# A three-layer kernel issued by its own list scheduler, with the order of its weight preparation changed

## The chip, the cores and the metric

The kernel runs on one core of a Trainium2 chip. The metric is the time of the whole program on the device in microseconds, as the median of several runs. The core has five engines that work side by side, each on its own queue in order: PE (matrix multiplication, with weight loads that overlap it), DVE and ACT (element-wise work), POOL, and SP, which issues the DMAs.

## The reference

Attention is a linear recurrence over 768 steps for 4 batches and 8 heads of width 48; its result is the input of two feed-forward layers over 3072 tokens.

```
mag = sqrt(a_re^2 + a_im^2);  scale = min(mag, 0.999) / (mag + 1e-6);  a = (a_re + i a_im) * scale
S_t = a_t * S_(t-1) + k_t v_t^T          # S: 48 x 48, complex, per batch and head
y_t = q_t^T re(S_t)
x  = y as (3072, 384)
x  = relu(x @ w_in)^2 @ w_out            # d_ff 2048
out = (silu(x @ w_gate) * (x @ w_val)) @ w_out2   # d_ff 1536
```

All inputs and outputs are float32.

## The kernel before

The sequence is cut into 6 chunks of 128 steps, 512 tokens each. For a chunk `attention` runs two generators: `elem` (DVE and ACT: normalisation, running products of a, scaled q and k called qs and ks, for two pairs of heads at a time) and `mat` (PE: transposes of ks and qs to kT and qT, copied by ACT; scores sc, masked by DVE to pb; py; the state). Its result goes by ACT (ys, L372) and DMA into xf. `moe1` splits xf into a high and a low part (xh, xl, L474 and L475) and then takes 16 column tiles of w_in: nine matmuls for h, Relu and Square (u), a rounded copy (gh, ACT), the remainder (gl, DVE L515), and two iterations later nine matmuls of `down` into acc. Products are made in three parts, high by high, high by low and low by high, so that float32 is kept on a faster matrix type. `moe2` does the same with two matrices (pg, pv), Silu on ACT and 12 iterations; its input comes back from DRAM through `input2`.

A weight tile is prepared by `wsplit`: read as integers (wst), three DVE operations (L400, L402, L404) put together the low part of wt, ACT rounds it into the first half (L413; DVE at L411 when `late` is set, that is for the second layer), POOL subtracts for the second half (L414), and ACT makes two flags of it (L417, L418). `prep1` does so for the 32 tiles of the first layer, `prep2` for the 36 of the second. Split tiles lie in 32 slots `w`, and in slots of attention's tiles when that is over (`wspare`); the integers are read into three buffers `pp`, which attention's pp and Bt share.

The order in which work is written is set by `drain`, which advances several generators in proportion: attention of chunk 0 together with `prep1`; then for each chunk `moe1` with the attention of the next one; for the last chunk `moe1` with `prep2`, which has first been advanced by its 8 spare slots; then `moe2` chunk by chunk. The framework's scheduler takes this as priority, orders the instructions of each engine by a model of its own, gives tiles their slots and sets all waits.

## Time and profile before

| | us |
|---|---|
| median of 3 runs (1225.9 to 1233.1) | 1231.74 |
| profiled execution, its own time | 1228.35 |
| span of the profiled execution | 1226.6 |
| PE busy | 1082.4 |
| DVE busy | 760.1 |
| ACT busy | 637.7 |
| POOL busy | 97.5 |

The span is from the first to the last instruction. Busy time is the time in which at least one instruction of the engine runs; as matmuls are pipelined and overlap, a busy PE is not PE at its peak. PEclk is the share of the matrix clock that was granted: 1.00 is 2.4 GHz and 0.50 is 1.2 GHz. In the stretches used below, 0 to 265 us holds attention of chunks 0 and 1 and the first layer of chunk 0; 265 to 374, 374 to 476, 476 to 579 and 579 to 685 the first layer of chunks 1 to 4, each with the attention of the next chunk; 685 to 772 the first layer of chunk 5; and then come six chunks of the second layer.

### The profile page before, as it was taken

How to read it: one execution, taken by the hardware profiler on the slowest of the kernel's cores; microseconds unless marked ns; L12 is line 12 of the kernel's file. 1: busy time of each engine (PE TensorE's matmuls, PEld its weight loads, DVE VectorE, ACT ScalarE, POOL GpSimd, SP SyncE). 2: the span in 40 equal slices, each digit the busy share in tenths (PEclk: the TensorE clock that was granted, in tenths of full speed). 3: DMA queues.
4: the chain of work that ended last, by engine and by line, in shares of the span. 5: the costliest groups of instructions: out<-in, count | busy, mean ns of one | idle time of the engine just before them, and what ended most of it. 6: DMA issues, size and time to landing. Idle time of an engine off the chain costs nothing.

```text
span 1226.6 us, 16542 instructions
## 1 busy us (share of the span) xinstructions
PE 1082.4 (88%) x5842; PEld 901.6 (74%) x5842; DVE 760.1 (62%) x1566; ACT 637.7 (52%) x1280; POOL 97.5 (8%) x75
## 2 busy tenths in 40 slices
PE   0346589989999999999999877999999999999997
PEld 0235467767777877878778655788898888888886
DVE  7987597968879879879788799223232232222221
ACT  4666777657677677777768666212122121221211
POOL 1231240000000000000003344000000000000000
PEclk9955599989999999999999999999999999999999
DMA  5353523142233332332334443101000010000000
GB/s 141 100 144 115 166 81 104 49 129 65 68 107 88 91 92 70 112 102 65 104 91 142 151 133 104 52 1 52 1 26 28 1 52 1 26 1 1 26 1 29
DMA packets 102492, 89.27 MB, mean 73 GB/s; under 512 B 35072, under 2 KB 90368, under 8 KB 102400
## 3 DMA queue, kind: packets, MB, share of 16 engines
q1 hardware_dynamic: 102400, 88.12, 24.5%
q8 instruction: 48, 0.79, 0.3%
q14 instruction: 44, 0.36, 0.1%
HBM read 64.49 MB, written 18.87 MB: 68 GB/s over the span
## 4 chain that ended last, share of the span: by engine, by line
PE 59%; DVE 22%; ACT 10%; issue 6%; DMA 2%; POOL 1%; SPq 0%; DVEq 0%; ACTq 0%; POOLq 0%
PE pg L483 4%; PE acc L558 4%; PE acc L556 4%; PE pg L484 4%; PE acc L557 4%; PE pg L482 4%; PE pv L483 4%; PE pv L482 4%; PE pv L484 4%; PE sc L348 3%; PE py L367 3%; PE pu L386 2%; PE acc L498 2%; PE acc L499 2%; DVE wt L402 2%
## 5 line engine op out<-in xcount | busy, mean ns | idle before, releaser
L569 DVE TENSOR_TENSOR u<-pv,u 128x512 f32<-128x512 f32 x72 | 49.8, 692 | 208.4 <-PE pv L484 208.4
L571 ACT CAST gh<-u 128x512 fp32r<-128x512 f32 x72 | 44.7, 620 | 217.0 <-PE acc L557 191.9
L482 PE MATMUL h<-xh,wc 128*128 128x512 f32 x288 | 117.6, 411 | 19.9 <-ACT xh L474 12.2
L498 PE MATMUL acc<-gl,wr 128*128 128x512 f32 x288 | 117.0, 406 | 20.3 <-DVE gl L515 20.1
L483 PE MATMUL h<-xl,wc 128*128 128x512 f32 x288 | 117.0, 406 | 5.7 <-DVE xl L475 5.7
L572 DVE TENSOR_TENSOR gl<-u,gh 128x512 fp32r<-128x512 f32 x72 | 49.8, 692 | 109.7 <-ACT gh L571 109.7
L497 PE MATMUL acc<-gh,wr 128*128 128x512 f32 x288 | 113.4, 403 | 4.6 <-ACT gh L514 4.6
L484 PE MATMUL h<-xh,wc 128*128 128x512 f32 x288 | 116.5, 405 | 0.0
L499 PE MATMUL acc<-gh,wr 128*128 128x512 f32 x288 | 114.5, 398 | 0.0
L414 POOL TENSOR_TENSOR wc<-wt,wc 128x384 fp32r<-128x384 f32 x40 | 58.7, 1466 | 573.0 <-DVE wc L411 506.8
L558 PE MATMUL acc<-wr,gl 128*128 128x384 f32 x288 | 97.0, 337 | 0.0
L556 PE MATMUL acc<-wr,gh 128*128 128x384 f32 x288 | 96.9, 336 | 0.0
L557 PE MATMUL acc<-wr,gh 128*128 128x384 f32 x288 | 96.7, 336 | 0.0
L568 ACT ACTIVATE u<-pg 128x512 f32<-128x512 f32 x72 | 43.0, 598 | 98.3 <-PE pg L484 98.3
L515 DVE TENSOR_TENSOR gl<-u,gh 128x512 fp32r<-128x512 f32 x96 | 74.4, 777 | 18.0 <-ACT gh L514 17.5
L483 PE MATMUL pg<-xl,wc 128*128 128x512 f32 x216 | 85.0, 394 | 0.0
L484 PE MATMUL pg<-xh,wc 128*128 128x512 f32 x216 | 85.0, 394 | 0.0
L483 PE MATMUL pv<-xl,wc 128*128 128x512 f32 x216 | 84.2, 390 | 0.0
L482 PE MATMUL pv<-xh,wc 128*128 128x512 f32 x216 | 84.1, 390 | 0.0
L482 PE MATMUL pg<-xh,wc 128*128 128x512 f32 x216 | 84.1, 389 | 0.0
L484 PE MATMUL pv<-xh,wc 128*128 128x512 f32 x216 | 84.0, 389 | 0.0
L498 PEld LDWEIGHTS acc<-gl,wr 128*128 128x128 f32 x288 | 54.3, 189 | 40.1 <-DVE gl L515 29.5
(131 smaller groups left out, 2482.6 us busy)
## 6 DMA issues: line engine op xcount, KB each, us to landing
wst<-in_moe_w_out_dram SPq DMA_DIRECT2D x28, 384.0 KB, 3.1
scr<-ks SPq DMA_DIRECT2D x24, 384.0 KB, 2.5
kn<-scr SPq DMA_DIRECT2D x24, 384.0 KB, 3.6
wst<-in_moe_w_in_dram SPq DMA_DIRECT2D x16, 384.0 KB, 3.9
in<-in_a_re_dram SPq DMA_DIRECT2D x96, 48.0 KB, 1.9
in<-in_a_im_dram SPq DMA_DIRECT2D x96, 48.0 KB, 1.9
in<-in_k_dram SPq DMA_DIRECT2D x96, 48.0 KB, 2.2
in<-in_q_dram SPq DMA_DIRECT2D x96, 48.0 KB, 2.0
```

The lines of the kernel that those rows point to most:

```text
L414: nc.gpsimd.tensor_tensor(out=dst[:, 1], in0=x, in1=dst[:, 0].bitcast(F32), op=ALU.subtract)
L482: nc.tensor.matmul(ps, w[:, 0, kd], xh[kd], start=kd == 0, stop=False)
L483: nc.tensor.matmul(ps, w[:, 0, kd], xl[kd], start=False, stop=False)
L484: nc.tensor.matmul(ps, w[:, 1, kd], xh[kd], start=False, stop=kd == self.KD - 1)
L497: nc.tensor.matmul(acc[d], w[:, 0, d], gh, start=i == 0, stop=False)
L498: nc.tensor.matmul(acc[d], w[:, 0, d], gl, start=False, stop=False)
L499: nc.tensor.matmul(acc[d], w[:, 1, d], gh, start=False, stop=i == NF - 1)
L515: nc.vector.tensor_tensor(out=gl, in0=u, in1=gh.bitcast(F32), op=ALU.subtract)
L556: nc.tensor.matmul(acc[t], gh[:, ts], f(0), start=i == 0, stop=False)
L557: nc.tensor.matmul(acc[t], gh[:, ts], f(1), start=False, stop=False)
L558: nc.tensor.matmul(acc[t], gl[:, ts], f(0), start=False, stop=i == NF - 1)
L569: nc.vector.tensor_tensor(out=u, in0=pv, in1=u, op=ALU.mult)
```

## The change

All calls of the main path go to a recorder (`Plan`), which notes each instruction's tiles, what it depends on and a duration from `weigh`. `arrange` then plays the engines forward in time: an engine that is free takes, of the instructions that are ready and whose tiles have a slot, the one that was recorded first; tiles of one tag get slots in the order of their recording. `issue` emits the instructions in the resulting order under `manual_schedule`, in which the framework keeps the given order and only sets the waits.

The recording order changes too. Attention of chunk 0 is recorded alone, except that after its first 5 steps 8 weight tiles are read ahead (`READ`, `LOADS`); the 32 splits come after it, one pair of tiles ahead of each iteration of moe1 on chunk 0 (`behind`), beside attention of chunk 1. 24 of the 32 reads go into slots of tag `w` itself, the last 8 into `pp`. For the second layer, 8 tiles are advanced as before, 16 are recorded beside moe1 of the last chunk (`EARLY`) and the rest beside moe2 of chunk 0. In `wsplit` ACT always makes the rounded copy and DVE subtracts in POOL's place; the last chunk's square goes from DVE to ACT; the output tile of moe2's fourth row block takes a buffer of gl.

```diff
--- before.py
+++ after.py
@@ -18,6 +18,265 @@
+class Engine:
+    def __init__(self, plan, engine, name):
+        self.plan, self.engine, self.name = plan, engine, name
+    def __getattr__(self, method):
+        call = getattr(self.engine, method)
+        return lambda *a, **kw: self.plan.record(self.name, method, call, a, kw)
...
+    def record(self, engine, method, call, args, kw):
+        names = self.POSITIONS.get(method, ("out", "in_"))
+        full = dict(zip(names, args))
+        full.update(kw)
+        aps = {k: v for k, v in full.items() if isinstance(v, bass.AP)}
+        o = Op()
+        i = len(self.ops)
+        o.call, o.args, o.kw, o.engine, o.rank = call, args, kw, engine, i
+        o.after, o.order, o.users, o.frees, o.tiles, o.ready, o.pair, o.size = set(), set(), [], [], [], 0.0, None, 0
+        self.ops.append(o)
+        for k, ap in aps.items():
+            h = ap.tensor
+            if not hasattr(h, "cap_key"):
+                continue
+            at, write = self.region(ap), k in self.OUTS
+            t = self.seen.setdefault(h.name, [h, [], None])
+            if engine == "tensor" and write:
+                if t[2] is not None:
+                    o.order.add(t[2])
...
+                    same = self.ops[j].engine == engine and engine != "sync"
+                    if same and (not w or engine == "tensor"):
+                        o.order.add(j)
+                    else:
+                        o.after.add(j)
...
+    def weigh(self, engine, method, full, aps):
+        out = aps["out"]
+        n = self.width(out)
+        if engine == "vector":
+            if method in ("tensor_scalar", "tensor_copy") and aps.get("in0", aps.get("in_")).space != bass.MemoryType.PSUM:
+                step = n / 1.92 + 70
+            elif method == "transpose":
+                step = n / 0.96 + 95
+            else:
+                step = n / 0.96 + 70
+            return step, step + 120
+        if engine == "scalar":
+            src = aps["in_"]
+            step = 0.833 * n + (55 if src.space == bass.MemoryType.PSUM else 88)
+            if "bias" in aps:
+                step += 100
+            if len(out.ap) > 2 and out.ap[-1][0] > 1:
+                step += 0.8 * n
+            if "accum_out" in aps:
+                step += 95
+            return step, step + 150
+        if engine == "tensor":
+            if method == "transpose":
+                return 109, 300
+            m = self.width(aps["lhsT"])
+            if aps["lhsT"].dtype == F32:
+                step = 2 * max(2 * n / 2.4 + 4, 0.87 * m)
+                return step, step + 190
+            step = n / 2.4 + 13.5
+            return step, step + 190
+        parts = out.ap[0][1] if out.space != bass.MemoryType.DRAM else aps["in_"].ap[0][1]
+        free = out if out.space != bass.MemoryType.DRAM else aps["in_"]
+        return 470, 2000 + 4 * parts * self.width(free) / 200.0
+    def arrange(self):
+        import heapq
+        ops, n = self.ops, len(self.ops)
...
+        while len(result) < n:
+            best = None
+            for e in engines:
+                if avail[e]:
+                    c = now[e]
+                elif pend[e]:
+                    c = max(now[e], pend[e][0][0])
+                else:
+                    continue
+                if best is None or c < best[0]:
+                    best = c, e
+            assert best, "no instruction can go on"
...
+            k, i = heapq.heappop(avail[e])
+            o = ops[i]
+            for name in set(o.tiles) - live:
+                g = tag_of[name]
+                if queue[g][at[g]] != name or not free[g]:
+                    wait = g, None
+                    break
...
+                if not warm:
+                    step, last = step * 1.9, last + step * 0.9
+                if o.pair and lastpair and o.pair[0] == lastpair[0] and o.pair[1] != lastpair[1]:
+                    now[e] -= 0
+                    step *= 0.06
...
+            if e in ("sync", "gpsimd"):
+                dma = max(dma, t) + (last - 2000)
+                end = max(t + 2000, dma + 1500)
+            else:
+                end = t + last
+            now[e] = t + step
+            o.ready = t
+            result.append((t, i))
...
+                u.ready = max(u.ready, (end + (60 if u.engine != e else 30)) if full else now[e])
+                u.need -= 1
...
+        self.span = max(now.values())
+        return [i for _, i in sorted(result)]
+    def issue(self):
+        order = self.arrange()
+        with self.tc.manual_schedule():
+            for i in order:
+                o = self.ops[i]
+                o.call(*o.args, **o.kw)
@@ -39,10 +298,15 @@
     AHEAD = 6
     AHEAD1 = 8
+    READ = 8
+    LOADS = 5
+    EARLY = 16
     def __init__(self, tc, q, k, v, a_re, a_im, w1, w2, wg, wv, wo, out):
         self.tc, self.nc = tc, tc.nc
         self.guard = False
-        self.late = False
         self.q, self.k, self.v, self.a_re, self.a_im = q, k, v, a_re, a_im
         self.w1, self.w2, self.wg, self.wv, self.wo, self.out = w1, w2, wg, wv, wo, out
         self.B, self.H, self.S, self.D = q.shape
@@ -407,11 +671,8 @@
         if self.guard:
             nc.vector.tensor_scalar(out=hi, in0=hi, scalar1=0x7FFFFFFF, scalar2=None, op0=ALU.bitwise_and)
             nc.vector.scalar_tensor_tensor(out=x, in0=hi.bitcast(F32), scalar=WLOW, in1=x, op0=ALU.is_ge, op1=ALU.mult)
-        if self.late:
-            nc.vector.tensor_copy(dst[:, 0], x)
-        else:
-            nc.scalar.copy(dst[:, 0], x)
-        nc.gpsimd.tensor_tensor(out=dst[:, 1], in0=x, in1=dst[:, 0].bitcast(F32), op=ALU.subtract)
+        nc.scalar.copy(dst[:, 0], x)
+        nc.vector.tensor_tensor(out=dst[:, 1], in0=x, in1=dst[:, 0].bitcast(F32), op=ALU.subtract)
         if not self.guard:
             hi = hi.bitcast(F32)
             nc.scalar.activation(out=hi, in_=hi, func=AF.Square, accum_out=self.flag(1))
@@ -425,31 +686,54 @@
         self.wlive += 1
         return self.wp.tile([128, 2, 3, 128], F32R, name=nm, tag="w", bufs=self.wbufs)
-    def w_col(self, src, i, dst):
-
-        st = self.e2.tile([128, 3, 256], I32, name="wst", tag="pp", bufs=self.NPP)
+    def stage(self, shape, own=False):
+        if own:
+            return self.wp.tile(shape, I32, name="wst", tag="w", bufs=self.wbufs)
+        return self.e2.tile(shape, I32, name="wst", tag="pp", bufs=self.NPP)
+    def read_col(self, src, i, own=False):
+        st = self.stage([128, 3, 256], own)
         self.nc.sync.dma_start(
             out=st, in_=src.bitcast(I32)[:, 256 * i:256 * i + 256].rearrange("(k p) f -> p k f", p=128))
-        dst[i] = t = self.wtile("wc")
-        self.wsplit(t.rearrange("p x k f -> p x (k f)"), st.rearrange("p k (f t) -> p (k f) t", t=2))
+        return st.rearrange("p k (f t) -> p (k f) t", t=2)
+    def read_row(self, src, i, own=False):
+        st = self.stage([128, 384, 2], own)
+        self.nc.sync.dma_start(out=st.rearrange("p f t -> p (f t)"), in_=src.bitcast(I32)[128 * i:128 * i + 128, :])
+        return st
+    def w_col(self, src, i, dst):
+        self.convert("wc", self.read_col(src, i), i, dst)
     def w_row(self, src, i, dst):
-        st = self.e2.tile([128, 384, 2], I32, name="wst", tag="pp", bufs=self.NPP)
-        self.nc.sync.dma_start(out=st.rearrange("p f t -> p (f t)"), in_=src.bitcast(I32)[128 * i:128 * i + 128, :])
-        dst[i] = t = self.wtile("wr")
+        self.convert("wr", self.read_row(src, i), i, dst)
+    def convert(self, name, st, i, dst):
+        dst[i] = t = self.wtile(name)
         self.wsplit(t.rearrange("p x k f -> p x (k f)"), st)
-    def prep1(self):
+    def prep1(self, ahead=0):
         self.w1t, self.w2t = {}, {}
-        for i in range(self.F1 // 128):
-            self.w_col(self.w1, i, self.w1t)
-            yield
-            self.w_row(self.w2, i, self.w2t)
+        todo = [x for i in range(self.F1 // 128) for x in (
+            (self.read_col, self.w1, i, "wc", self.w1t), (self.read_row, self.w2, i, "wr", self.w2t))]
+        own = len(todo) - ahead if ahead else 0
+        read = []
+        for j in range(-1, len(todo)):
+            while len(read) < len(todo) and len(read) <= j + ahead:
+                f, src, i, _, _ = todo[len(read)]
+                if len(read) >= own and len(read) > j:
+                    break
+                read.append(f(src, i, len(read) < own))
+            if j >= 0:
+                _, _, i, name, dst = todo[j]
+                self.convert(name, read[j], i, dst)
             yield
     def prep2(self):
-        self.late = True
         self.wgt, self.wvt, self.wot = {}, {}, {}
         for i in range(self.F2 // 128):
             for f, src, dst in ((self.w_col, self.wg, self.wgt), (self.w_col, self.wv, self.wvt),
@@ -506,10 +790,7 @@
             u = self.mp.tile([128, N], F32, name="u", tag="u", bufs=self.NU)
             gl = self.mp.tile([128, N], F32R, name="gl", tag="gl", bufs=self.N_gl)
             nc.scalar.activation(out=u, in_=ps, func=AF.Relu)
-            if final:
-                nc.vector.tensor_tensor(out=u, in0=u, in1=u, op=ALU.mult)
-            else:
-                nc.scalar.activation(out=u, in_=u, func=AF.Square)
+            nc.scalar.activation(out=u, in_=u, func=AF.Square)
             gh = self.mp.tile([128, N], F32R, name="gh", tag="gh", bufs=self.N_gh)
             nc.scalar.copy(gh, u)
             nc.vector.tensor_tensor(out=gl, in0=u, in1=gh.bitcast(F32), op=ALU.subtract)
@@ -581,7 +862,8 @@
             down(*p)
         L = 32 * nb
         for t in range(nb):
-            o = self.mp.tile([128, self.DM], F32, name="o", tag="u", bufs=self.NU)
+            tag, bufs = ("u", self.NU) if t < 3 else ("gl", self.N_gl)
+            o = self.mp.tile([128, self.DM], F32, name="o", tag=tag, bufs=bufs)
             if t % 2:
                 nc.scalar.copy(o, acc[t])
             else:
@@ -617,7 +899,8 @@
                 yield
     @staticmethod
-    def drain(*its):
+    def drain(*its, until=None):
         its = [[it, 0, k] for it, k in its]
         while its:
@@ -627,6 +910,8 @@
                 next(e[0])
                 e[1] += 1
             except StopIteration:
+                if e[0] is until:
+                    return
                 its.remove(e)
     def xtile(self, n):
@@ -636,22 +921,42 @@
         NC = len(self.chunks)
         drain, NATT = self.drain, self.NATT
         xf = self.xtile(0)
-        drain((self.attention(0, xf), NATT), (self.prep1(), 2 * self.F1 // 128))
+        first, w1 = self.attention(0, xf), self.prep1(self.READ)
+        for _ in range(self.LOADS):
+            next(first)
+        next(w1)
+        drain((first, NATT))
         for n in range(NC):
-            its = [(self.moe1(n, xf), 2 * self.F1 // 128)]
+            m = self.moe1(n, xf)
+            its = [(self.behind(w1, m) if n == 0 else m, 2 * self.F1 // 128)]
             if n + 1 < NC:
                 xf = self.xtile(n + 1)
                 its.append((self.attention(n + 1, xf), NATT))
+                drain(*its)
             else:
                 self.wspare = [(self.e2, t, getattr(self, "N_" + t)) for t in ("qs", "ks", "kn", "qT", "kT")] + [
                     (self.ld, "in2", self.NIN)] * self.NIN
                 p2 = self.prep2()
                 for _ in range(len(self.wspare)):
                     next(p2)
-                its.append((p2, 3 * self.F2 // 128))
-            drain(*its)
-        for n in range(NC):
+                drain((m, 2 * self.F1 // 128), (p2, self.EARLY), until=m)
+        m = self.moe2(0)
+        drain((m, 2 * self.F2 // 128), (p2, 3 * self.F2 // 128))
+        for n in range(1, NC):
             drain((self.moe2(n), 24))
+    @staticmethod
+    def behind(first, then):
+        while True:
+            for _ in range(2):
+                next(first, None)
+            for _ in range(2):
+                try:
+                    next(then)
+                except StopIteration:
+                    return
+                yield
     def steps(self, ctx, ys):
@@ -751,7 +1056,10 @@
         with ExitStack() as c2:
             k.pools(c2)
             k.constants(c2)
+            k.nc = plan = Plan(tc)
             k.fast()
+            plan.issue()
+            k.nc = tc.nc
         with ExitStack() as c2:
             vp = c2.enter_context(tc.tile_pool(name="vp", bufs=1, space=PSUM))
             v2 = c2.enter_context(tc.tile_pool(name="v2", bufs=1))
```

## Rows read from the trace of the kernel before

**Rows 1.** The page, part 1: engine, busy us, share of the span, instructions.

```profile
PE 1082.4 (88%) x5842; PEld 901.6 (74%) x5842; DVE 760.1 (62%) x1566; ACT 637.7 (52%) x1280; POOL 97.5 (8%) x75
```

**Rows 2.** Busy time of each engine by stretch: stretch, length, then per engine.

```profile
0.00:265.00 265.00, 162.90 (x908) 128.45 (x908) 213.08 (x469) 177.20 (x395) 51.30 (x39) 0.83 0.40 114
...
47.00:102.00 55.00, 25.95 (x142) 20.00 (x142) 49.87 (x111) 37.38 (x90) 17.75 (x10) 0.62 0.49 143
265.00:374.00 109.00, 102.22 (x615) 81.38 (x615) 91.03 (x208) 74.33 (x137) 0.00 (x0) 0.97 0.32 85
374.00:476.00 102.00, 99.32 (x625) 81.61 (x624) 86.67 (x203) 74.00 (x139) 0.00 (x0) 1.00 0.32 88
476.00:579.00 103.00, 100.51 (x629) 82.00 (x628) 86.76 (x199) 76.47 (x145) 0.00 (x0) 1.00 0.31 87
579.00:685.00 106.00, 102.07 (x632) 82.61 (x631) 85.44 (x176) 77.62 (x159) 9.85 (x8) 1.00 0.40 122
685.00:772.00 87.00, 68.14 (x281) 51.54 (x280) 82.47 (x140) 56.08 (x140) 36.32 (x28) 1.00 0.38 121
772.00:846.00 74.00, 74.00 (x359) 65.24 (x359) 19.32 (x29) 18.19 (x30) 0.00 (x0) 1.00 0.06 22
```

**Rows 3.** The timeline at three hand-overs: start us, length us, engine, line.

```profile
116.83 0.95 DVE L308 TENSOR_TENSOR ks<-pp,pm 128x768 f32<-128x768 f32 x1
...
140.83 0.60 ACT L474 CAST xh<-xf 128x512 fp32r<-128x512 f32 x1
...
264.38 0.20 ACT L372 ACTIVATION_READ_ACCUMULATOR ys<-py 48x1 f32 x1
```

**Rows 4.** Groups of instructions, 0 to 215 us: busy us, mean ns, idle before.

```profile
L404 DVE SCALAR_TENSOR_TENSOR wt<-wst,wt 128x384 int32<-128x384 int32 x32 | 21.0, 656 | 0.2
...
L400 DVE TENSOR_SCALAR wt<-wst 128x384 int32<-128x384 int32 x32 | 14.5, 453 | 9.9 <-DMA wst<-in_moe_w_in_dram 8.3 <-POOL wc L414 0.9 <-DMA wst<-in_moe_w_out_dram 0.7
```

**Rows 5.** The timeline, 133 to 140 us: split operations packed on DVE and ACT.

```profile
133.10 0.35 DVE L400 TENSOR_SCALAR wt<-wst 128x384 int32<-128x384 int32 x1
133.37 0.55 DVE L404 SCALAR_TENSOR_TENSOR wt<-wst,wt 128x384 int32<-128x384 int32 x1
133.84 0.55 DVE L402 SCALAR_TENSOR_TENSOR wt<-wst,wt 128x384 int32<-128x384 int32 x1
...
137.71 0.53 ACT L417 ACTIVATE wst<-wst 128x384 f32<-128x384 f32 x1
...
138.24 0.49 ACT L413 CAST wc<-wt 128x384 fp32r<-128x384 f32 x1
138.64 0.64 ACT L418 ACTIVATE wst<-wst,wlow 128x384 f32<-128x384 f32 x1
...
139.27 0.54 ACT L417 ACTIVATE wst<-wst 128x384 f32<-128x384 f32 x1
```

**Rows 6.** The timeline, 700 to 704 us, in the last chunk's first layer.

```profile
700.25 0.39 PE L482 MATMUL h<-xh,wc 128*128 128x512 f32 x1
...
700.48 0.39 PE L483 MATMUL h<-xl,wc 128*128 128x512 f32 x1
...
701.17 1.25 POOL L414 TENSOR_TENSOR wc<-wt,wc 128x384 fp32r<-128x384 f32 x1 [1.64 <-DVE wc L411]
701.48 1.49 DVE L515 TENSOR_TENSOR gl<-u,gh 128x512 fp32r<-128x512 f32 x1
...
703.02 0.50 PE L498 MATMUL acc<-gl,wr 128*128 128x512 f32 x1 [1.68 <-DVE gl L515]
```

**Rows 7.** Groups of instructions, 374 to 579 us, without work on POOL.

```profile
L515 DVE TENSOR_TENSOR gl<-u,gh 128x512 fp32r<-128x512 f32 x32 | 21.9, 685 | 7.4 <-ACT gh L514 7.4
L512 ACT ACTIVATE u<-u 128x512 f32<-128x512 f32 x32 | 20.2, 630 | 0.6
...
L223 DVE TENSOR_TENSOR an<-in,z 128x384 f32<-128x384 f32 x16 | 8.4, 553 | 0.2
```

**Rows 8.** Groups of instructions, 760 to 846 us, around the first Silu.

```profile
L568 ACT ACT_TABLE_LOAD x1 | 1.3, 1283 | 1.5 <-PE pg L484 1.5
```

125 lines of the change are left out of this document (added).

## The prediction

> **What bounds the kernel now.** I read the first part of the page, then the stretches between the stages, then in each stretch the rows of whichever engine is short. The page alone misleads: PE is busy 88% of the span [rows 1], so little seems left. The stretches [rows 2] show three regimes. In 772 to 846, one chunk of the second layer, PE is busy 74.00 of 74 us while DVE and ACT have under 20 us each: six such chunks fill the rest of the span (454.6 us); they are pure PE time, and nothing in a new order shortens them. From 265 to 685, four chunks, PE is busy 102.2 of 109, 99.3 of 102, 100.5 of 103 and 102.1 of 106 us: nearly bound. But in the first 265 us PE has only 162.9 us of work, and in 685 to 772 (first layer of the last chunk) 68.1 of 87. What is short there is DVE: 213.1 of 265 and 82.5 of 87 us.
>
> Why DVE is short differs. In front it has two jobs at once, attention of chunks 0 and 1 and the splitting of 32 weight tiles. The last ks of chunk 0 is written at 116.83, its x is taken up at 140.83, and attention of chunk 1 ends only at 264.38 [rows 3], so the second chunk can't start before 265. In the last chunk DVE's time is partly not work: while POOL subtracts for 1.25 us, the DVE operation gl that starts 0.3 us later takes 1.49 us, and a matmul behind it waits 1.68 us [rows 6]; the same gl takes 685 ns where POOL has nothing to do [rows 7].
>
> **The change part by part.** The profiled execution took 1228.35 us, 1226.6 us of span and 1.75 around it; the median of the runs, 1231.74, lies 3.4 above it. I sum against the former and add 3.4 at the end.
>
> *The subtraction moves from POOL to DVE, the late cast and the final square from DVE to ACT.* Steps, from start to start where DVE is packed [rows 5]: the first operation of a split 0.27 us (133.10 to 133.37), the second kind 0.47 (133.37 to 133.84). A moved subtraction has the shape of the L223 product, 553 ns [rows 7] against 550 for L404 in [rows 5], so also a step of 0.47. A weight tile then costs DVE 0.27 + 3 x 0.47 = 1.68 us, and ACT 1.56 us: L417 0.53, the cast 0.40, L418 0.63 with the reads of their sums (137.71, 138.24, 138.64, 139.27 [rows 5]). What DVE gets back is blocking: L404 averages 656 ns and L400 453 in the front [rows 4], against 0.55 and 0.35 clean [rows 5], so 32 x (0.106 + 0.103) = 6.7 us on these two lines. POOL's queue is empty afterwards; nobody is behind it.
>
> *Attention of chunk 0 first, weights behind it (the front).* DVE's work until attention 1 is done: 213.1 as busy now [rows 2], + 32 x 0.47 = 15.0 for the subtractions, - 6.7 unblocked = 221.4 us. How much idle time lies between? From above, the present share: 213.1 / 265 = 80%, giving 275 (10 lost). From below, none: 221, and 5 us for the first loads, 226 (39 won). I take 49.87 / 55 = 91%, the stretch 47 to 102 [rows 2], which is the nearest: attention and weight splits mixed, each filling the other's waits. It gives 244, so **21 us won**. One reason against 80%: 8.3 of the 9.9 us that DVE idles ahead of L400 ended with the landing of a weight read [rows 4]. Weights are staged in three buffers shared with pp and Bt; the change reads eight ahead into the weights' own slots. Those eight reads are moved on SP's queue past the k and q loads of chunk 0, at some 0.4 us of issue each and 3.0 MB in all; at the 143 GB/s of 47 to 102 [rows 2] that is 21 us of transfer before k and q are wanted, about 30 us in. I cost it at nothing; if it isn't covered, up to 5 us, inside the bounds. Attention 0 itself, no longer queued behind splits, should hand over its x some 20 us before 140.83 (an estimate: a dozen splits of 1.7 us), and its gaps go to splits and to attention 1.
>
> *The list scheduler over chunks 1 to 4.* The work is the same, only its order changes; no row of before shows the new order. The bound on the good side: all of PE's idle time goes, 6.8 + 2.7 + 2.5 + 3.9 = 16 us [rows 2], and the granted clock of 0.97 in 265 to 374 becomes 1.00, 3 us; some more from attention matmuls that now run behind late copies, say 30 in all. On the bad side, a list made from modelled steps waits where the engines disagree with it: I allow 10 lost. I take **17 won**, near the first sum, since the two stretches that hold most of it (109 and 106 us against 102) are disturbed by things the change removes: a late attention 1 with a clock dip, and eight weight splits with POOL in chunk 4 (9.9 us of POOL there [rows 2]).
>
> *Second-layer weights over two chunks.* Of 36 tiles 8 are read ahead as now, 16 instead of 28 go beside the first layer of chunk 5, and 12 beside the first four iterations of moe2 on chunk 0. In chunk 5, per iteration: PE 18 matmuls at 0.23 us (700.25 to 700.48 [rows 6]) = 4.1; DVE 1.68 + 0.6 for gl = 2.3. ACT has 56.1 us now [rows 2]; it loses the flags of 12 tiles (12 x 1.16), gains 16 squares of 0.63 (L512 [rows 7]) and 16 casts of 0.40 [rows 5]: about 59 of 16 x 4.1 + 6 = 72 us, the 6 for the first operand and the last copies. So PE binds: 87 becomes 72, **15 won** (6 if ACT's order delays gh and gl, 19 if moe2's first matmuls fill the last gaps). In moe2 on chunk 0 an iteration has 74 / 12 = 6.2 us of PE [rows 2]; with three tiles DVE has 3 x 1.68 + 1.4 = 6.4, ACT 3 x 1.56 + 1.2 = 5.9. DVE is late by 0.2 us in each of four iterations and is in order: **3 lost** (0 to 10).
>
> Sum: 21 + 17 + 15 - 3 = 50; 1228.35 - 50 = 1178, + 3.4 = **1181 us** as a median.
>
> **The rivals.**
>
> *PE alone binds (better).* If splits and attention 1 fit under the first chunk, PE never starves after 118: 118 + five chunks of 99.3 + 68.1 [rows 2] = 683, then the 454.6 us from 772 to the end unchanged: 1138, + 5 = 1143. For it: with 12 of the 32 splits done by 118, DVE has 1.68 x 20 + 87 (its busy time in a chunk [rows 2]) = 121 us left against PE's 99, so a quicker start is not far from it. Against: the other 22 us have to go somewhere, and in no stretch of attention in [rows 2] is DVE idle for under 9%.
>
> *The gain is given back.* Front idle stays at 80% (-10), chunks 1 to 4 don't move, moe2 on chunk 0 is late by 10, chunk 5 wins 15: about 1236. For it: moe1 of chunk 0 now waits for each split tile instead of finding 32 ready.
>
> *The list doesn't do what it says.* The framework's scheduler already fills gaps by priority; if each engine's order comes out nearly the same, only the hand-written parts count: chunk 5 and half of the front, 15 + 10 - 3: 1210.
>
> *Slower.* Queues are in order. In chunks 0 to 4, PE takes some 64 operands per chunk from ACT or DVE right after they are made (kT, qT, pb, gh, gl), 320 hand-overs. Where the list has put a matmul too early, PE waits with ready matmuls behind it, and ACT and DVE wait for PE's result in turn. At a mean lateness t this costs 320 t: from t = 0.16 us it eats the 50 us, and from 0.2 the kernel is over 1% slower; at 0.22, 1252. Against it: the list's figures agree with rows here (a 512-wide matmul 226.8 ns against the step of 0.23, a weight tile's three ACT operations 503, 408 and 603 against 0.53, 0.40 and 0.63 [rows 5, 6]), and PE idles only 2.5 us in a whole chunk under the present order, which is also made ahead of time. For it: PE's clock, granted at 0.62 in 47 to 102 and 0.97 in 265 to 374 [rows 2], is guessed in the list by an account of its own, and at the lower level its matmuls end much later than listed.
>
> *Table loads.* Squares and Relus of the weight flags now stand between Silus. A load of a table takes 1283 ns on ACT and there is one ahead of the first Silu [rows 8]; casts behind it need none. If Square is not in Silu's table, 12 tiles cost up to two loads each, 12 x 2 x 1.28 = 31 us of ACT in four iterations that have no slack: 1212. The Trainium skill, ScalarE: Activation LUTs, section Table sets, says that functions are loaded in named sets and that cheap ones, relu, copy, identity and abs, are in every set; it doesn't list Square there, and no row of before shows a Square behind that load.
>
> **How the numbers follow.** Forecast (some 1160 to 1205) 0.58; PE alone 0.15; table loads 0.03; list of no effect 0.05; given back 0.12; slower 0.07. About 1% is what a measurement of this kernel tells from no change (1219.4 and 1244.1). Faster holds the first four, 0.81; same 0.12; slower 0.07. The range leaves out the two last: up to 1218, and down to 1143 where the rival of PE alone stands.
>
> **What would show it.** POOL without tile work, and no gl over 0.75 us. Attention 0's last ks before 105 and moe1's first relu near 120. Attention 1 ending near 244 with DVE busy over 88% until then; below 83% the front's step is wrong. Chunk periods of 100 to 102 us, and PE's idle share there not above the present 2 to 4%: more, with releases by ACT or DVE, is the slower rival. Chunk 5 near 72 us with PE over 92% busy. Two table loads in all. The prediction fails most likely on the front, where the 91% is chosen, and on chunks 1 to 4, where nothing of the new order can be seen beforehand.

## The result, and the profile after

| | median, us | lowest to highest | ratio to before, 95% interval |
|---|---|---|---|
| before | 1229.36 | 1225.9 to 1233.1 | |
| after | 1174.39 | 1171.52 to 1177.37 | 0.9553 [0.9508, 0.9598] |

The profiled execution of the changed kernel took 1172.15 us, its span is 1170.1. Every instruction of the main path now bears the line of `issue`, L279 (another where lines were removed), so the reader goes by tiles. The page's first line, against [rows 1]:

```profile
PE 1054.8 (90%) x5842; PEld 892.8 (76%) x5842; DVE 728.9 (62%) x1582; ACT 656.2 (56%) x1332; POOL 0.9 (0%) x7
```

PE is busy 28 us less, DVE 31 us less, although DVE now makes 68 subtractions, and POOL has nothing left to do. The stretches between the same events as in [rows 2]: attention 1 and the first layer of chunk 0 done (256), the first layer of chunks 1 to 5, the second layer of chunk 0.

```profile
0.00:256.00 256.00, 152.48 (x914) 119.83 (x914) 220.04 (x519) 179.41 (x400) 0.94 (x7) 0.88 0.43 122
...
256.00:353.00 97.00, 95.32 (x612) 79.69 (x613) 79.50 (x180) 71.75 (x133) 0.00 (x0) 1.00 0.32 89
353.00:450.00 97.00, 97.00 (x623) 81.55 (x622) 79.57 (x185) 73.56 (x136) 0.00 (x0) 1.00 0.31 87
450.00:549.00 99.00, 99.00 (x630) 82.55 (x629) 81.64 (x188) 74.15 (x137) 0.00 (x0) 1.00 0.32 89
549.00:647.00 98.00, 98.00 (x626) 81.80 (x625) 81.00 (x188) 71.99 (x138) 0.00 (x0) 1.00 0.31 92
647.00:715.00 68.00, 66.25 (x288) 53.53 (x287) 54.25 (x111) 65.28 (x168) 0.00 (x0) 1.00 0.51 160
715.00:789.00 74.00, 74.00 (x359) 65.31 (x358) 37.78 (x70) 36.64 (x86) 0.00 (x0) 1.00 0.25 78
```

Chunks 1 to 4 take 97 to 99 us each and PE is never idle in three of them (97.00 of 97.00, 99.00 of 99.00, 98.00 of 98.00); before they took 102 to 109. The last chunk's first layer takes 68 us in place of 87. The front, 256 us, moved little, and PE, busy for 152.5 us of it, still starves there. What it waits for stands in the timeline around 85 to 130 us (start, length, engine, instruction, idle time before it and what ended it):

```profile
85.07 0.35 DVE L279 TENSOR_SCALAR wt<-wst 128x384 int32<-128x384 int32 x1
...
90.41 0.62 DVE L279 TENSOR_SCALAR wt<-wst 128x384 int32<-128x384 int32 x2
...
125.61 0.62 ACT L279 ACTIVATE lp<-pm,tiny 128x384 f32<-128x384 f32 x1 [1.43 <-DVE pm L279]
...
126.49 0.35 DVE L279 TENSOR_SCALAR wt<-wst 128x384 int32<-128x384 int32 x1
...
129.21 0.51 ACT L279 CAST wc<-wt 128x384 fp32r<-128x384 f32 x1 [2.43 <-DVE wt L279]
...
129.78 0.80 PE L279 MATMUL h<-xh,wc 128*128 128x512 f32 x1 [11.17 <-ACT wc L279]
```

Four weight tiles are begun by 91 us, and then none for 35 us: the next one (126.49) starts right after attention 1 has taken its own pm and lp (125.61). PE meanwhile stood idle for 11.17 us for the next wc. What ends last in the front has changed with this: attention of chunk 1 is over at 219.7 us, the last of the 32 splits begins at 243.95, and the first layer of chunk 0 is copied out at 255.5.

```profile
219.50 0.20 ACT L279 ACTIVATION_READ_ACCUMULATOR ys<-py 48x1 f32 x1
...
243.95 0.35 DVE L279 TENSOR_SCALAR wt<-wst 128x384 int32<-128x384 int32 x1
...
253.92 1.54 ACT L279 COPY x<-acc 128x512 f32<-128x512 f32 x3
```

The times of the stages in this and the later runs, in us, read from the timelines as the end of the last copy x<-acc of a chunk (for after: 255.5 us for chunk 0, 352.6 for chunk 1) and of the third copy o<-acc of the second layer:

| kernel | to the end of chunk 1 | chunks 2 to 4 | chunk 5 | second layer, chunk 0 | span |
|---|---|---|---|---|---|
| before | 374.3 | 310.5 | 87.3 | 74.1 | 1226.6 |
| after | 352.6 | 294.4 | 68.3 | 73.4 | 1170.1 |
| f1_subtract_alone | 364.0 | 308.0 | 74.5 | 73.5 | 1200.2 |
| e3_moves_only | 359.2 | 308.3 | 71.5 | 78.0 | 1197.2 |
| e1_framework_order | 373.9 | 309.6 | 67.4 | 73.4 | 1206.5 |
| e2_old_sequence | 357.7 | 295.0 | 70.6 | 74.1 | 1177.5 |
| f2_flat_figures | 367.8 | 370.9 | 104.1 | 72.5 | 1295.2 |
| g3_list_always_warm | 365.1 | 294.4 | 68.3 | 73.4 | 1182.6 |
| f3_early_28 | 353.9 | 294.5 | 69.9 | 72.2 | 1171.7 |
| e5_wt_two_slots | 347.6 | 294.6 | 68.6 | 77.3 | 1168.0 |
| e4_wt_one_slot | 388.1 | 296.9 | 73.0 | 78.4 | 1217.7 |
| f4_old_sequence_wt_slots | 361.0 | 294.2 | 69.3 | 76.6 | 1181.0 |
| g2_no_read_ahead | 365.4 | 296.3 | 70.5 | 77.1 | 1189.3 |
| g4_attention1_slower | 348.2 | 297.5 | 69.0 | 74.2 | 1170.1 |

### The profile page after: what moved, and what is told of

It is laid out like the page before. It is cut to its first block, busy times and chain, and to the rows that moved or that the text cites. A ratio compares the mean times of both kernels' runs of the same rounds, so it can differ in the third digit from the quotient of the medians.

```text
span 1170.1 us, 16337 instructions
## 1 busy us (share of the span) xinstructions
PE 1054.8 (90%) x5842; PEld 892.8 (76%) x5842; DVE 728.9 (62%) x1582; ACT 656.2 (56%) x1332; POOL 0.9 (0%) x7
## 4 chain that ended last, share of the span: by engine, by line
PE 77%; ACT 10%; DVE 9%; issue 1%; DMA 1%; SPq 1%; DVEq 0%; ACTq 0%
PE acc L279 25%; PE pg L279 13%; PE pv L279 13%; PE h L279 12%; PE py L279 4%; PE pt L279 3%; PE sc L279 3%; ACT wst L279 3%; PE pu L279 3%; DVE AB L279 1%; ACT u L279 1%; DVE wt L279 1%; SPq L279 1%; DVE pp L279 1%; ACT gh L279 1%
## 5 line engine op out<-in xcount | busy, mean ns | idle before, releaser
L279 ACT CAST gh<-u 128x512 fp32r<-128x512 f32 x168 | 103.9, 619 | 220.2 <-PE acc L279 195.0
L279 PE MATMUL h<-xh,wc 128*128 128x512 f32 x576 | 203.5, 406 | 25.7 <-ACT wc L279 19.9
L279 PE MATMUL acc<-gh,wr 128*128 128x512 f32 x576 | 202.2, 406 | 6.9 <-ACT gh L279 6.9
L279 DVE TENSOR_TENSOR gl<-u,gh 128x512 fp32r<-128x512 f32 x168 | 115.7, 689 | 117.5 <-ACT gh L279 116.7
L279 DVE TENSOR_TENSOR u<-pv,u 128x512 f32<-128x512 f32 x72 | 49.7, 691 | 191.9 <-PE pv L279 189.6
L279 PEld LDWEIGHTS h<-xh,wc 128*128 128x128 f32 x576 | 109.2, 192 | 52.6 <-ACT wc L279 21.8
L279 PE MATMUL acc<-wr,gh 128*128 128x384 f32 x576 | 147.3, 336 | 0.0
L279 PE MATMUL pg<-xh,wc 128*128 128x512 f32 x432 | 145.9, 392 | 0.0
L279 PE MATMUL pv<-xh,wc 128*128 128x512 f32 x432 | 144.9, 390 | 0.0
L279 PEld LDWEIGHTS acc<-gh,wr 128*128 128x128 f32 x576 | 108.8, 192 | 30.6 <-ACT gh L279 9.6
L279 PE MATMUL h<-xl,wc 128*128 128x512 f32 x288 | 116.0, 403 | 2.2 <-DVE xl L279 2.2
L279 PE MATMUL acc<-gl,wr 128*128 128x512 f32 x288 | 115.6, 402 | 0.3 <-DVE gl L279 0.2
L279 PEld LDWEIGHTS acc<-wr,gh 128*128 128x128 f32 x576 | 105.6, 188 | 4.7
L279 ACT ACTIVATE u<-pg 128x512 f32<-128x512 f32 x72 | 43.0, 598 | 98.2 <-PE pg L279 97.6
L279 PE MATMUL acc<-wr,gl 128*128 128x384 f32 x288 | 97.1, 337 | 0.0
L279 PEld LDWEIGHTS pv<-xh,wc 128*128 128x128 f32 x432 | 81.2, 188 | 17.3
L279 PEld LDWEIGHTS pg<-xh,wc 128*128 128x128 f32 x432 | 81.2, 188 | 15.5
L279 PE MATMUL pt<-ident,ks 128*96 128x128 f32 x192 | 31.3, 288 | 64.5 <-DVE ks L279 63.5
L279 PE MATMUL pg<-xl,wc 128*128 128x512 f32 x216 | 85.1, 394 | 0.0
L279 PE MATMUL pv<-xl,wc 128*128 128x512 f32 x216 | 84.3, 390 | 0.0
L279 ACT ACTIVATE u<-h 128x512 f32<-128x512 f32 x96 | 57.1, 595 | 40.7 <-PE h L279 38.3
L279 PEld LDWEIGHTS pt<-ident,ks 128*96 128x96 f32 x192 | 22.9, 135 | 68.4 <-issue 64.4
```

The costliest lines, as they stand in the source:

```text
L279: o.call(*o.args, **o.kw)
```

## The experiments

Three things changed together: the moves between engines, the sequence in which work is recorded, and who orders it. The first four runs part them. My theory after the result was that the list shortens chunks 1 to 4 and the sequence does the rest; the rival was that the moves did most.

**Framework's order, new sequence, moves.**

```diff
-            k.nc = plan = Plan(tc)
             k.fast()
-            plan.issue()
-            k.nc = tc.nc
```

> The new recording order and the moves between engines, but ordered by the framework's scheduler as before. If the list is what shortened chunks 1 to 4 (105 to 98 us each), these chunks come back to 102 us or more and the time is 1195 to 1205. If sequence and moves did it, chunks stay near 98 and the time is 1170 to 1180.

1206.55 us, 0.9797 [0.9759, 0.9834]. Chunks 2 to 4 went back to 309.6 us, as expected of the list. But the front went back entirely, 373.9 to the end of chunk 1, with PE waiting for split tiles in 100 to 270 us about as long as in the changed kernel (19.7 us, see below). These waits alone thus do not explain it (engine, what it waits for: us in total, times, longest):

```profile
PE h L766 <- ACT wc L674: 21.6, 6, 12.8
```

**List, old sequence, moves.** `fast` is that of the kernel before; everything else is the changed kernel.

```diff
-        first, w1 = self.attention(0, xf), self.prep1(self.READ)
...
+        drain((self.attention(0, xf), NATT), (self.prep1(), 2 * self.F1 // 128))
...
```

> The list scheduler and the moves between engines, but recorded in the old sequence (attention 0 beside the 32 splits, all second-layer weights beside the last first-layer chunk). If the list acts by itself, chunks 1 to 4 stay near 98 us; the front goes back to 265 or more and the last chunk to 75 to 80 us: 1185 to 1200. If list and sequence only work together, 1220 or more.

1179.1 us, 0.9581 [0.9551, 0.9612], less than either theory gave it: the front went back by 5 us only, and the last chunk by 2. The list keeps its gain in chunks 2 to 4 under either sequence, 13 us here (308.3 to 295.0) and 15 under the new one (309.6 to 294.4). The interval overlaps that of the changed kernel; the traces differ by 5.1 us at the end of chunk 1. Stretches of chunks 2 to 4, first with the framework's order (the next run, moves alone), then with the list's:

```profile
359.00:667.00 308.00, 299.67 (x1878) 245.59 (x1878) 254.69 (x572) 229.13 (x448) 0.00 (x0) 1.00 0.35 100
```

```profile
358.00:653.00 295.00, 294.56 (x1875) 245.50 (x1874) 243.45 (x557) 218.82 (x412) 0.00 (x0) 1.00 0.32 90
```

Same 1875 to 1878 matmuls; PE idle 8.3 us under the one, 0.4 under the other, and its busy time is 5 us shorter too.

**Moves alone.** The kernel before, in which DVE subtracts and ACT makes every cast and the last square.

```diff
-        if self.late:
-            nc.vector.tensor_copy(dst[:, 0], x)
-        else:
-            nc.scalar.copy(dst[:, 0], x)
-        nc.gpsimd.tensor_tensor(out=dst[:, 1], in0=x, in1=dst[:, 0].bitcast(F32), op=ALU.subtract)
+        nc.scalar.copy(dst[:, 0], x)
+        nc.vector.tensor_tensor(out=dst[:, 1], in0=x, in1=dst[:, 0].bitcast(F32), op=ALU.subtract)
...
```

> The kernel before with only the moves: DVE subtracts in place of POOL, ACT makes every rounded copy and the last square. If POOL's blocking of DVE was what stretched the last chunk, it falls from 87 to 72 to 76 us and the time to 1210 to 1218. If DVE's added work takes the place of the blocking, the time stays within 1% of 1229.

1198.75 us, 0.9752 [0.9724, 0.9779]: 31 of the 55 us, without list or sequence, and more than either theory gave it. Which of the moves it was:

**The subtraction alone.**

```diff
-        nc.gpsimd.tensor_tensor(out=dst[:, 1], in0=x, in1=dst[:, 0].bitcast(F32), op=ALU.subtract)
+        nc.vector.tensor_tensor(out=dst[:, 1], in0=x, in1=dst[:, 0].bitcast(F32), op=ALU.subtract)
```

> The kernel before with one line changed: DVE subtracts in POOL's place; late casts and the last square stay on DVE. If POOL's blocking of DVE is what the moves to DVE and ACT cured (31 us together), this alone gives 20 to 31 us: 1199 to 1210. If unloading DVE by 36 casts and 16 squares (some 20 us of DVE time) was it, this gives under 10: 1220 or more.

1198.06 us, 0.9755 [0.9716, 0.9795]: one word in the source gives all of it. Two stretches, and groups of 0 to 160 us against [rows 4] (one L404 falls outside):

```profile
0.00:255.00 255.00, 168.14 (x905) 133.90 (x906) 210.44 (x500) 177.29 (x395) 0.94 (x7) 0.91 0.42 119
...
672.00:747.00 75.00, 71.15 (x308) 56.91 (x306) 73.78 (x169) 54.24 (x141) 0.00 (x0) 1.00 0.43 133
...
L404 DVE SCALAR_TENSOR_TENSOR wt<-wst,wt 128x384 int32<-128x384 int32 x31 | 17.1, 550 | 0.1
...
L400 DVE TENSOR_SCALAR wt<-wst 128x384 int32<-128x384 int32 x32 | 11.3, 354 | 3.3 <-DMA wst<-in_moe_w_in_dram 2.3 <-DMA wst<-in_moe_w_out_dram 0.8
```

By 255 us this kernel is where the one before was at 265 (chunk 1 ends 10.3 us sooner). DVE was busy 210.4 us until then, with 32 subtractions more in it, against 213.1. So 213.1 + 15.0 - 210.4 = 17.7 us of blocking went (the mean durations of the groups in both stretches give 15.5), not the 6.7 that two lines show: L402 had 1.6 us more, and the rest had lain on attention's operations that happened to meet POOL.

Blocking is not the whole of the front's gain, though. DVE's work there fell by only 2.7 us; the other 7 of the 10 us are idle time of DVE, 44.6 us in place of 51.9, and ahead of L400 alone, where it mostly waits for a weight read, 3.3 in place of 9.9 [rows 4]. Why that wait shrank isn't shown. In the last chunk the balance closes: DVE falls from 82.5 to 73.8 us with 28 subtractions more, and the chunk from 87 to 75. The two operations that were blocked most there, before (685 to 772) and with the subtraction on DVE (672 to 747):

```profile
L510 DVE TENSOR_TENSOR u<-u 128x512 f32<-128x512 f32 x16 | 20.8, 1298 | 0.0
L515 DVE TENSOR_TENSOR gl<-u,gh 128x512 fp32r<-128x512 f32 x16 | 19.8, 1236 | 0.6 <-ACT gh L514 0.4
```

```profile
L515 DVE TENSOR_TENSOR gl<-u,gh 128x512 fp32r<-128x512 f32 x16 | 10.9, 682 | 0.0
L510 DVE TENSOR_TENSOR u<-u 128x512 f32<-128x512 f32 x16 | 10.9, 682 | 0.0
```

The Trainium skill, SBUF — State Buffer, section SBUF: two separate sides, says that GpSimd and DVE share a pair of SBUF ports under an exclusive lock: of a GpSimd instruction and a DVE instruction in a two-port mode, or with two SBUF inputs while GpSimd reads SBUF, the one that starts first holds the pair for its whole length and the other blocks. The traces agree: gl took 1.49 us beside POOL [rows 6], and nowhere over 0.7 us here.

**Do the list's figures matter?** Every DVE and ACT instruction is listed at 500 ns, every matmul at 180, without clock and pairing.

```diff
+        if engine in ("vector", "scalar"):
+            return 500, 600
+        if engine == "tensor":
+            return 180, 370
...
```

> The changed kernel with a list made from flat figures: every DVE and ACT instruction 500 ns, every matmul 180 ns, no clock, no pairing. If the list wins by its figures (hand-overs that come when listed), PE's idle time comes back in chunks 1 to 4, which go from 98 to 101 to 105 us, and the time is 1185 to 1200. If any order by recording with ready operands first does it, it stays within 6 us of 1174. If lateness were as dear as the rival had it (over 0.16 us at 320 hand-overs), it is over 1220.

1293.2 us, 1.0513 [1.046, 1.0565]: slower than the kernel before. Under this sequence the calibrated list gives 32 us (1206.55 to 1174.39); the flat one costs 87. The place is one stretch behind the first layer of each of chunks 1 to 4, not a little everywhere. In 283 to 368 us the first layer of chunk 1 runs, in 368 to 405 what is left of the attention of chunk 2, and the first layer of chunk 2 begins only then. The two stretches, and a wait in the second:

```profile
283.00:368.00 85.00, 81.69 (x443) 66.76 (x444) 55.48 (x133) 54.46 (x100) 0.00 (x0) 0.98 0.19 51
...
368.00:405.00 37.00, 24.29 (x180) 20.34 (x179) 28.31 (x59) 22.12 (x39) 0.00 (x0) 0.79 0.45 124
```

```profile
PE pt L255 <- DVE ks L255: 8.4, 1, 8.4
```

In the first stretch PE runs the layer's matmuls at full pace while DVE works only 55.5 of 85 us on the attention that the next chunk needs; in the second that layer is done, and PE has 24.3 us of work in 37, at a granted clock of 0.79. The list has put the two kinds of work on PE in a wrong proportion. Which of the figures does it isn't shown.

**A list without its account of the clock.** `if not warm` becomes `if False`.

> The changed kernel with a list that takes PE's clock as always full. If the list's account of the clock matters, the front, where 0.83 to 0.92 was granted, is ordered worse: 1178 or more. If figures of single instructions and not the clock's account were what the flat list lacked, it stays within 4 us of 1174, chunks 1 to 4 at 98 us.

1184.58 us, 0.963 [0.9596, 0.9665]. Chunks 2 to 4 are as in the changed kernel to 0.1 us; the front is 12.5 us longer:

```profile
0.00:267.00 267.00, 161.29 (x914) 127.16 (x914) 220.33 (x517) 177.85 (x400) 0.94 (x7) 0.87 0.42 116
...
365.00:561.00 196.00, 196.00 (x1251) 164.10 (x1250) 161.32 (x372) 147.69 (x273) 0.00 (x0) 1.00 0.32 88
```

So the account counts where the clock really falls (0.87 granted in the front here), and nowhere else.

**Second-layer weights beside one chunk again.** `EARLY = 28` in place of 16.

> The changed kernel with all 28 remaining second-layer tiles recorded beside the first layer of the last chunk again. ACT then has 12 x 1.56 = 19 us more there: 65 + 19 = 84 against 68 us. If spreading is needed now that ACT does casts and squares, that chunk takes 80 to 85 us and the second layer's first chunk stays at 74: 1184 to 1190. If greedy filling spreads the flags by itself, the sum of both chunks stays within 4 us of 142.

1174.49 us, 0.9569 [0.9528, 0.9611], no difference. ACT's work in the last chunk is 67.2 us, not 84: operations of the last tiles were taken into the next chunk by readiness, whatever was recorded.

```profile
648.00:718.00 70.00, 68.10 (x296) 54.78 (x295) 55.88 (x114) 67.19 (x173) 0.00 (x0) 1.00 0.52 162
718.00:790.00 72.00, 72.00 (x350) 63.55 (x349) 36.03 (x67) 35.16 (x80) 0.00 (x0) 1.00 0.23 72
```

**The front: slots of their own for wt.** The rule that tiles of one tag take slots in recorded order makes wt wait behind pm and lp of attention. Two slots for wt, two in place of three for pm and lp:

```diff
-    NSMK = 3
+    NSMK = 2
...
-        t = self.e2.tile([128, 384], I32, name="wt", tag="smk", bufs=self.NSMK)
+        t = self.e2.tile([128, 384], I32, name="wt", tag="wt", bufs=2)
```

> The changed kernel with two slots of its own for wt and two in place of three for pm and lp. If the splits of the front were held back because wt took its slots behind pm and lp of attention in recorded order, splits start near 15 us instead of 82, PE's waits for wc (20 us) go, and the time falls by 8 to 15 us to 1160 to 1166. If DVE's total work sets the front, it stays within 4 us of 1174; with attention short of slots, it could rise by some us.

1165.44 us, 0.9471 [0.9437, 0.9505], the fastest of all; its interval lies just below that of the changed kernel. Splits start at 12 us:

```profile
0.00:251.00 251.00, 160.10 (x913) 126.39 (x914) 214.25 (x515) 177.99 (x397) 0.94 (x7) 0.88 0.44 123
...
0.00:82.00 82.00, 28.18 (x142) 23.00 (x142) 66.09 (x174) 47.04 (x104) 0.94 (x7) 0.89 0.57 164
...
12.36 0.35 DVE L279 TENSOR_SCALAR wt<-wst 128x384 int32<-128x384 int32 x1
...
13.22 0.35 DVE L279 TENSOR_SCALAR wt<-wst 128x384 int32<-128x384 int32 x1
```

The same 913 or 914 matmuls are done by 251 us instead of 256, and PE idles for 90.9 us among them instead of 103.5. Its waits for wc in the first layer of chunk 0, first in the changed kernel (106 to 256 us), then here (110 to 251):

```profile
PE h L279 <- ACT wc L279: 19.7, 3, 11.2
```

```profile
PE h L279 <- DVE wc L279: 3.4, 2, 3.0
PE h L279 <- ACT wc L279: 2.2, 1, 2.2
```

The way is not quite the one expected: in 0 to 82 us DVE is as busy as before (66.1 us here, 66.0 in the changed kernel), so the splits did not fill idle time there; they displaced attention 0, whose last ks moved from 87 to 101 us, and that is less than the wait for wc was worth. In the trace the second layer's chunk 0 gives back 3.9 of the 5 us won by the end of chunk 1 (77.3 against 73.4), which was not followed up; the profiled execution, 1170.09 us, lies above the median.

**One slot for wt, three for pm and lp.** As above with `bufs=1` and `NSMK = 3`.

> The changed kernel with one slot of its own for wt and the three for pm and lp kept. If what counts is that wt doesn't stand in the line of pm and lp, it comes to 1163 to 1169 like two slots (1165). If one slot makes splits follow each other with their full delay (some 3 us a tile, 96 us in all, inside the front's 250), a few us more: up to 1172. If attention's third slot was worth something, under 1163.

1212.08 us, 0.9846 [0.98, 0.9893]: a miss. Being out of attention's line isn't enough.

```profile
110.00:289.00 179.00, 142.19 (x685) 110.54 (x685) 145.07 (x344) 121.86 (x280) 0.00 (x0) 0.79 0.32 88
...
PE acc L279 <- ACT gh L279: 15.6, 7, 2.8
...
PE h L279 <- DVE wc L279: 0.7, 2, 0.5
PE h L279 <- ACT wc L279: 0.6, 2, 0.4
```

The 32 tiles begin between 12 and 280 us, one every 8.6 us where I had put 3 (with two slots, one every 7.3). My reading is that each of a tile's steps takes its turn on DVE and ACT and that with one slot nothing overlaps them. How this costs PE so much isn't shown: it waits for wc for only 1.3 us here, but for 15.6 for gh, and its granted clock is 0.79, against 0.92 with two slots in 110 to 251.

**Old sequence with these slots.** The run with the old sequence, and two slots for wt.

> The list scheduler with the old sequence and wt in two slots of its own, two for pm and lp. The new sequence was worth 5 us with shared slots. If its use is that splits fill attention 0's gaps, and the shared slots hid that, the difference to the new sequence with the same slots (1165) grows to 8 or more: 1173 to 1182. If free slots make both sequences the same for a list that takes whatever is ready, it comes to 1163 to 1170.

1183.83 us, 0.9644 [0.9602, 0.9687]: 18 us above the new sequence with the same slots. With slots of its own for wt the sequence counts, and 13 of the 18 us lie in the front (361.0 against 347.6 to the end of chunk 1).

**No reads ahead.** `prep1(0)` in place of `prep1(self.READ)`, with two slots for wt: each read goes into pp's buffers.

> Two slots for wt, but no weight read ahead: each read goes into the three buffers shared with pp and Bt, recorded with its split. If the reads ahead into the weights' own slots are a part of the gain, splits can't start before attention 0's last pp is taken (near 80 us), as with wt in the shared line: 1174 or more. If only wt's slots held splits back, it stays at 1165.

1193.4 us, 0.9709 [0.967, 0.975], 28 us lost. The first split starts at 84.92, as with wt in the shared line, and PE's waits for split tiles run on through the layer:

```profile
84.92 0.35 DVE L279 TENSOR_SCALAR wt<-wst 128x384 int32<-128x384 int32 x1
...
PE h L279 <- ACT wc L279: 13.1, 5, 4.2
```

**Attention 1 recorded more slowly.** `NATT if n else 125`, with two slots for wt.

> Two slots for wt, and attention of chunk 1 recorded at 125/150 of its pace beside the first layer of chunk 0. With two slots attention 1 ends near 224 and chunk 0 near 251, both fed by DVE. If DVE's work is simply spread wrongly between them, both end near 240 and the time is 1155 to 1161. If a late attention 1 is paid back in chunk 1, it stays at 1163 to 1168.

1171.72 us, 0.952 [0.9484, 0.9555]: above both forecasts. Nothing was won in the front, 348.2 against 347.6 to the end of chunk 1, and 3 us were lost in chunks 2 to 4. At this one pace, at least, sharing DVE otherwise between the two gains nothing.

## Why the prediction held, point by point

The total was near (1181 forecast, 1174.39 measured; 50 us forecast, 56.2 between the profiled executions), the terms less so, and in part it was luck: the sum took the subtraction's move as 15.0 - 6.7 = 8.3 us more work for DVE in the front and put the gain there on the new sequence; measured alone, the move gives 30 us (1228.46 to 1198.06) and the sequence nothing that the times resolve.

*The front, 21 us won:* 9.5 (265 to 255.5). Two steps failed. The first is the path: the front was to end with attention 1, near 244 us, but attention 1 was over at 219.7, and the first layer of chunk 0 ended last, at 255.5, waiting for its weights. The second is the idle share: 91% busy was taken, 220.0 of 256 is 86%. The reason was in the diff and in my own description of it: splits could not fill attention 0's gaps, because wt shares its line of slots with pm and lp. That 221.4 us of work were forecast and 220.0 measured is luck: 15.5 to 17.7 us of blocking went and not 6.7, and 0 to 256 holds 19 DVE instructions more than the 500 of the subtraction alone by 255, 9.6 us, nearly all of them attention of chunk 2. By the runs, the subtraction gave 10 us here, the new sequence nothing that the times resolve under the list (5.1 us in the traces), and 15 us lost under the framework's order (373.9 against 359.2). There too PE waits for wc, 21.6 us against 19.7 in the changed kernel; what makes its front so much longer was not followed up.

*Chunks 1 to 4, 17 won:* 28 (419.8 to 391.5), inside the bound of 30. Of the 16 in chunks 2 to 4, 13 are the list's alone (308.3 to 295.0), by PE's idle time as the sum had it and by 5 us of PE time besides; the 12 of chunk 1 (109.3 to 97.1) were not taken apart.

*Last chunk, 15 won:* 19.0, the upper bound. PE binds, as costed (66.3 of 68 us), but it isn't the spreading: with 28 tiles beside it the chunk and its successor take as long. The subtraction gave 12.8 of it.

*Second layer, chunk 0, 3 lost:* 0.7 won. DVE and ACT have 37.8 and 36.6 us in 74; the 12 tiles were not dense enough to delay PE.

*The rivals.* Table loads: refuted; Squares and Relus of the flags stand between Silus, and there is one load, of 1283 ns as in [rows 8].

```profile
L279 ACT ACTIVATE wst<-wst,wlow 128x384 f32<-128x384 f32 x11 | 7.2, 654 | 0.2
...
L279 ACT ACT_TABLE_LOAD x1 | 1.3, 1283 | 0.0
```

The Trainium skill, ScalarE: Activation LUTs, section Table sets, names relu, copy, identity and abs as functions of every set, and not Square; here no load came behind a Square. *PE alone* (1143) failed in the front, where PE idled for 103.5 of 256 us. *The gain is given back* had its premise right, since moe1 of chunk 0 did wait for split tiles, but the chunks behind it won 28 us and not nothing. *Slower* was right in kind: figures decide whether the list gains or loses. But its mechanism was not lateness at 320 hand-overs: the flat list lost 76 us in chunks 2 to 4 (370.9 against 294.4) and 36 in chunk 5, in one stretch each. *The list doesn't do what it says* is refuted by chunks 2 to 4 (308 against 295). What the page showed of POOL beforehand, 8% busy, was the largest single cause, and I priced it by the two lines nearest to it instead of by all DVE operations that can meet it.

## What to carry to other kernels

Where DVE is short, work on POOL is not free: price it by the DVE time that it blocks, on every line that can meet it, and, since waits change too, try the move by itself before anything larger. A list scheduler is as good as its figures and its rule for slots: calibrate durations from a trace, and give work that should fill gaps its own buffers, since one shared line of slots is an order that no priority can change; two won 9 us here, while a single one lost 38. Take changes apart after they succeed: of three parts, the moves gave over half (31 of 55 us), the list most of the rest (1198.75 to 1179.1 under the old sequence), and the new sequence nothing that the times resolve until wt had slots of its own.

## What had not been expected of the hardware

The price of one POOL operation: 68 subtractions, 97.5 us of POOL and 8% of the span, cost 30 us of 1228 where DVE was the short engine. A DVE operation with a single tensor input was held as well: L400, 354 ns mean once POOL was empty, 453 before. And under the list PE ran 294 us (353 to 647) with no idle time between matmuls of two kinds of work, at a granted clock of 1.00.
